# Sixteen partitions between the batch rows of a decode kernel's final sum, and two stacked copies in place of two side-by-side ones

## The chip, the cores and the metric

The kernel runs on one core of one Trainium2 chip. The metric is device time in microseconds (us) of the whole launch: the median over several runs. A profile covers one execution, and its span is the part of that execution in which the profiler saw instructions. TensorE is PE in the profile (PEld is its weight load), VectorE is DVE, ScalarE is ACT, GpSimd is POOL, SyncE is SP.

## The reference, cut to what matters

Two batch rows `x` of 448 values are normalized and go through an attention layer over the last 4096 positions of a long cache (16 query heads, 8 key/value heads of 256) and, next to it, through a dense layer with a mish activation. The result is the sum of three terms, two rows of 448 values:

```python
x = A_x                                  # 2 x 1 x 448, bfloat16
xn = _layernorm(x, axis=-1)
return x + _A_ref(xn, A_k_cache, A_v_cache, A_wq, A_wo) + _B_ref(xn, B_w1, B_b1, B_w2)
# _A_ref: q = xn @ wq;  p = softmax(q k^T / 16);  o = p v;  o (2 x 4096) @ wo (4096 x 448)
# _B_ref: h = xn @ w1 + b1;  act = h * tanh(softplus(h));  act (2 x 1792) @ w2 (1792 x 448)
```

## The kernel before

**Stages.** The work order is written out by hand in the body of the kernel (lines 651 to 743); no scheduler reorders it. Nearly all loads are issued by SP, in program order. First come `wq`, the first two key blocks (`load_k`, 4 MB each) and `w1`. `project` (L324) forms the queries, and the VectorE copies at L361 spread them into `qd`. Then a loop `u` over four groups of heads runs `turns` (VectorE transposes of the key block, L306), `scores` (TensorE, L393; ScalarE exponential, L401), `values` (TensorE, L439), `gather`, `finish`, `relay` and `mix_early`. The key, value, `wq` and `w2` blocks share a ring of three buffers, so a load waits until the block that lay there is used up.

**Set-up.** Before the first key block is transposed, GpSimd fills constants in program order (`ident`, `qd`, `ones`, `hot`, `pick_f`, `xs`, the `sp` tiles, `w2_x`), and VectorE makes small tables from `ident`, among them `id2`, a 2 x 2 identity in float32 (L145, L146).

**The final sum.** For the first three groups, the products with `wo` are added in `early` (2 x 448 in PSUM). For the last group and for the dense output the sum lies in `acc`, a PSUM tile of 224 columns: the left 224 output columns of the two batch rows lie on partitions 0 and 1, the right 224 on partitions 32 and 33. `carry` (L271) copies `early` to SBUF and brings it into `acc` through `id2`. `add_rows` (L284) issues one pair of matmuls for each 128 rows of weights, one into partitions 0 and 1 and one into 32 and 33; the stationary operand has two columns (batch rows), the moving operand 224 columns of weights. `mix` (L527) makes eight pairs from `ox` and `wo`; `dense_out` (L643) makes thirteen pairs from `act_bf` and `w2`. `w2` comes in five parts (`w2_parts`, L626), and the pairs of each part wait for that part. `relay` (L493) writes `ox`: in the last group ScalarE writes its partitions 0 to 63 and VectorE 64 to 127.

**The end.** After the last pair, VectorE copies partitions 0 and 1 and ScalarE partitions 32 and 33 of `acc` into the two halves of `res` (2 x 448, bfloat16), and SP stores `res` as two runs of 896 bytes:

```python
    res = consts.tile([Bsz, D], BF16)
    for g in range(SG):
        dst = res[:, g * SD : (g + 1) * SD]
        src = acc[32 * g : 32 * g + Bsz, :]
        if g % 2 == 0:
            nc.vector.tensor_copy(out=dst, in_=src)
        else:
            nc.scalar.copy(out=dst, in_=src)
    nc.sync.dma_start(out=out.flatten_outer_dims(), in_=res[:])
```

Of the kernel before, what the change touches and what calls it, by code (L numbers as in the profile page):

```python
# [9 lines left out]
ALU = mybir.AluOpType  # L10
AXIS = mybir.AxisListType
BF16 = mybir.dt.bfloat16
FP32 = mybir.dt.float32
# [4 lines left out]
def kernel(  # L18
# [13 lines left out]
    nc = tc.nc  # L32
    P = 128
# [5 lines left out]
    Bsz, Sq, D = A_x.shape  # L39
# [8 lines left out]
    U = Hkv // KU  # L48
# [13 lines left out]
    NI = F2 // P  # L62
    NR = NI - 1
# [16 lines left out]
    consts = ctx.enter_context(tc.tile_pool(name="consts", bufs=1))  # L80
    small = ctx.enter_context(tc.tile_pool(name="small", bufs=2))
# [46 lines left out]
    for lo, hi in ((0, HW // 2), (HW // 2, NS * HW // 2), (NS * HW // 2, NS * HW)):  # L128
# [6 lines left out]
    ident = consts.tile([P, P], BF16)  # L135
# [6 lines left out]
    nc.vector.tensor_copy(  # L142
        out=halves[:], in_=ident[0:2, 0:2].unsqueeze(2).to_broadcast([2, 2, Bsz])
    )
    id2 = consts.tile([Bsz, Bsz], FP32)  # L145
    nc.vector.tensor_copy(out=id2[:], in_=ident[0:Bsz, 0:Bsz])  # L146
    hot = consts.tile([P, KU, 4, rep, 32, KU], BF16)
    nc.gpsimd.memset(hot[:], 0.0)
    for k in range(KU):
        nc.gpsimd.tensor_copy(  # L150
            out=hot[:, k, :, :, :, k],
            in_=ident[:].rearrange("p (q y) -> p y q", y=4).unsqueeze(2)
# [11 lines left out]
        out=rstd[:], in_=mv[:, 1:2], func=ACT.Sqrt, bias=eps_t[:], scale=1.0  # L164
# [4 lines left out]
        out=xn_bf[:],  # L169
        in0=x_bf[:],  # L170
# [7 lines left out]
        out=parm[:], in_=ident[:].rearrange("p (a o) -> p o a", o=2), axis=AXIS.X, op=ALU.add  # L178
# [3 lines left out]
        out=jm[:],  # L182
        in_=ident[:].rearrange("p (a j h) -> p j a h", j=J, h=rep),
        axis=AXIS.XY,
        op=ALU.add,
    )
    nc.vector.tensor_scalar(
        out=jm[:], in0=jm[:], scalar1=-1.0, scalar2=29952.0, op0=ALU.add, op1=ALU.mult
# [3 lines left out]
        out=mneg[:], in_=jm[:].unsqueeze(1).to_broadcast([P, TH * 8, J])  # L192
    )
    sel = consts.tile([P, 2, NQ], FP32)
    for x in range(2):
        for w in range(4):
            at = 32 * w + (2 * (w % 2) + x) * NQ
            src = ident[:, at : at + NQ]
            if w == 0:
                nc.vector.tensor_copy(out=sel[:, x, :], in_=src)  # L200
            else:
                nc.vector.tensor_tensor(
                    out=sel[:, x, :], in0=sel[:, x, :], in1=src, op=ALU.add
# [9 lines left out]
        out=pick_f[0:QB, 0:12],  # L213
        in_=idb.rearrange("p (a s) -> p a s", s=XB),
        axis=AXIS.X,
        op=ALU.add,
    )
    nc.vector.tensor_reduce(
        out=pick_f[QB:P, XO:XP].rearrange("p (e r) -> p e r", r=4)[:, :, 0:2],
        in_=ida.rearrange("p (e r s) -> p e r s", r=2, s=XA),  # L220
        axis=AXIS.X,
        op=ALU.add,
    )
    nc.vector.tensor_reduce(
        out=pick_f[QB:P, XP : XP + XA],
        in_=ida.rearrange("p (a s) -> p s a", s=XA),
        axis=AXIS.X,
        op=ALU.add,
    )
    nc.vector.tensor_reduce(  # L230
        out=pick_f[0:QB, XP:],
        in_=idb.rearrange("p (a s) -> p s a", s=XB),
        axis=AXIS.X,
        op=ALU.add,
# [18 lines left out]
    for odd in range(2):  # L253
        for half in range(2):
            o = (half + odd) % 2
            nc.vector.tensor_scalar(
                out=xs[:, odd::2, half * Bsz : (half + 1) * Bsz],
                in0=xr_ps[:, odd::2, :],
# [9 lines left out]
    SG, SD = 2, D // 2  # L268
    acc = ps_a.tile([P, SD], FP32)

    def carry():  # L271
        e_sb = small.tile([P, 2 * Dh], FP32, tag="vs", name="e_sb", bufs=1)[0:Bsz, 0:D]
        nc.scalar.copy(out=e_sb, in_=early[:])
        for g in range(SG):
            nc.tensor.matmul(
                acc[32 * g : 32 * g + Bsz, :],
                lhsT=id2[:],
                rhs=e_sb[:, g * SD : (g + 1) * SD],
                start=True,
                stop=False,  # L280
                skip_group_check=True,
            )

    def add_rows(lhsT, rows, stop=False):  # L284
        for g in range(SG):
            nc.tensor.matmul(  # L286
                acc[32 * g : 32 * g + Bsz, :],
                lhsT=lhsT,
                rhs=rows[:, g * SD : (g + 1) * SD],
                start=False,  # L290
                stop=stop,
                skip_group_check=True,
            )
# [20 lines left out]
    for n in range(2):  # L314
        for e in range(2):
# [3 lines left out]
                out=sp[:],  # L319
                in_=ident[:, o : o + 63 : 2].unsqueeze(1).to_broadcast([P, G, 32]),  # L320
# [91 lines left out]
    state = {}  # L412
# [80 lines left out]
    def relay(u):  # L493
        oT = state.pop(("oT", u))
        ox_ps = ps_m.tile([P, 4, 2, rep, Bsz], FP32, tag="m", name="ox_ps")
        for y in range(4):
            for k in range(KU):
                nc.tensor.matmul(  # L498
                    ox_ps[:, y, :, :, :].rearrange("p c h b -> p (c h b)"),
                    lhsT=hot[:, k, y, :, :, :].rearrange("p h q k -> p (h q k)"),  # L500
                    rhs=oT[:, :, k * rep : (k + 1) * rep, :].rearrange("p c h b -> p c (h b)"),
                    start=(y == 0 and k == 0),
                    stop=(y == 3 and k == KU - 1),
                    skip_group_check=True,
                )
        ox = small.tile([P, 8, Bsz], BF16, tag="ox", name="ox")
        for h in range(rep):
            rows = slice(h * 64, (h + 1) * 64)
            copy = nc.vector.tensor_copy if u == U - 1 and h == 1 else nc.scalar.copy
            copy(  # L510
                out=ox[rows].rearrange("p (y c) b -> p y c b", c=2), in_=ox_ps[rows, :, :, h, :]
            )
        state["ox", u] = ox
# [11 lines left out]
            )  # L525

    def mix(u):  # L527
        ox = state.pop(("ox", u))
        w = wo_t.pop(u)[:].rearrange("p k h (c d) -> p (k h c) d", c=2)
        for i in range(8):  # L530
            add_rows(ox[:, i, :], w[:, i, :])

    act_bf = consts.tile([P, NI, 2, Bsz], BF16)
    dealt = consts.tile([P, XS, Bsz], BF16)
    act_x = consts.tile([XP, XS, Bsz], BF16)
    w2_x = consts.tile([XP, XS * D], BF16)
# [34 lines left out]
    def mish():  # L571
        h_ps = state.pop("h")
        shape = [P, NI, 2, Bsz]
        u_sb = consts.tile(shape, FP32, name="u_sb")
        nc.scalar.activation(out=u_sb[:], in_=h_ps[:], func=ACT.Exp)
        t_sb = consts.tile(shape, FP32, name="t_sb")
        nc.vector.scalar_tensor_tensor(
            out=t_sb[:], in0=u_sb[:], scalar=2.0, in1=u_sb[:], op0=ALU.add, op1=ALU.mult
        )
        den = consts.tile(shape, FP32, name="den_sb")  # L580
        nc.vector.tensor_scalar(
            out=den[:], in0=t_sb[:], scalar1=2.0, scalar2=None, op0=ALU.add
        )
        nc.vector.reciprocal(out=den[:], in_=den[:])
        nc.vector.tensor_tensor(out=t_sb[:], in0=t_sb[:], in1=den[:], op=ALU.mult)
        nc.vector.tensor_tensor(out=act_bf[:], in0=h_ps[:], in1=t_sb[:], op=ALU.mult)
        nc.vector.tensor_tensor(
            out=dealt[:],
            in0=act_bf[:, NR, 1, :].unsqueeze(1).to_broadcast([P, XS, Bsz]),
            in1=share[:].unsqueeze(2).to_broadcast([P, XS, Bsz]),  # L590
            op=ALU.mult,
        )
# [50 lines left out]
    def dense_out(part):  # L643
        k, lo, hi = w2_parts[part]
        for i in range(lo, hi):
            at = k * KH + i * D
            add_rows(
                act_bf[:, i, k, :], state["w2"][:, at : at + D], stop=(k == 1 and i == NR - 1)
            )

    load_w1()
# [18 lines left out]
    turns(0, 1)  # L670
    dense_in()
    mish()
    scores(0, 1)
    weigh(0)
    regroup()
    for u in range(U - 1):
        load_k(u + 1, 0)
        load_v(u, 0)
        load_k(u + 1, 1)
        load_v(u, 1)  # L680
        load_wo(u)
        if u == 0:
            load_xb(0)
            load_xb(1)
            load_xa(0)
        if u == 1:
            load_xb(2)
            load_xb(3)
            load_xa(1)
        turns(u + 1, 0)  # L690
        values(u, 0)
        scores(u + 1, 0)
        turns(u + 1, 1)
        if u == U - 2:
            pace(11, key=ktm[1][:, 0, 0, :, 0:16])
        values(u, 1)
        gather(u)
        finish(u)
        scores(u + 1, 1)
        relay(u)  # L700
        if u == U - 2:
            dense_x()
        mix_early(u)
        if u < U - 2:
            weigh(u + 1)
    u = U - 1
# [5 lines left out]
    for part in range(len(w2_parts)):  # L712
        load_w2(part)
    pace(3)
    carry()
    pace(5)
    values(u, 0)
# [9 lines left out]
    pace(1)  # L727
    finish(u)
    relay(u)
    pace(2)  # L730
    mix(u)
    for part in range(len(w2_parts)):
        dense_out(part)

    res = consts.tile([Bsz, D], BF16)
    for g in range(SG):
        dst = res[:, g * SD : (g + 1) * SD]
        src = acc[32 * g : 32 * g + Bsz, :]
        if g % 2 == 0:
            nc.vector.tensor_copy(out=dst, in_=src)  # L740
        else:
            nc.scalar.copy(out=dst, in_=src)
    nc.sync.dma_start(out=out.flatten_outer_dims(), in_=res[:])


# [28 lines left out]
```

## Time and profile before

| | us |
|---|---|
| median of 3 runs | 188.88 (188.82 to 189.43) |
| the profiled execution | 188.59 |
| its span | 186.8 |
| PE busy, share of the span | 88.9, 48% |
| DVE busy | 97.1, 52% |
| ACT busy | 12.6, 7% |
| POOL busy | 7.8, 4% |
| bytes moved | 77.78 MB, 416 GB/s over the span |
| last copies of `acc`, DVE L740 and ACT L742 | 0.377 and 0.337 |
| issue of the store, L743 | 0.273, from 184.81 |

The profiled execution is 1.8 us longer than its span, and 0.29 us below the median. Times inside the span are counted from its start. An entry of the timeline gives start, length, engine, line, operation, the tiles written and read, the shapes, and in brackets how long the engine was idle before it and what ended that.

### The profile page before, as it was taken

The page shows a single profiled execution, that of the slowest core. Times are in us where ns is not written, and L with a number is a line of the kernel's source. Part 1 is how long each engine was busy: PE and PEld are TensorE (multiplying, and loading weights), DVE is VectorE, ACT ScalarE, POOL GpSimd, SP SyncE. Part 2 cuts the span into 40 slices and gives each one's busy share as a digit, 9 for nine tenths or more (in the row PEclk, how much of TensorE's full clock was granted, in tenths as well). Part 3 has the DMA queues.
Part 4 walks back from the last instruction along what each step waited for, and adds up shares of the span by engine and source line. Part 5 has one row for each costly group of instructions (what it writes and reads, how often), then busy time and mean ns, then how long its engine had stood idle before and what let it go on. Part 6 is the DMA issues. An engine that isn't in the chain of part 4 may idle for free.

```text
span 186.8 us, 1974 instructions
## 1 busy us (share of the span) xinstructions
PE 88.9 (48%) x854; PEld 38.1 (20%) x854; DVE 97.1 (52%) x100; ACT 12.6 (7%) x27; POOL 7.8 (4%) x18
## 2 busy tenths in 40 slices
PE   0057015893209300783039101881059059899694
PEld 0022002541003100241013000330022013434353
DVE  6961798974792098028940296048920593040100
ACT  3004000101000100110000100110000000210100
POOL 8800000000000000000000000000000000000000
PEclk9999999955555855599555855798556756999999
DMA  6999999999999999999999999999999999999991
GB/s 207 442 475 442 407 435 405 452 446 444 414 421 421 432 449 389 472 442 442 414 435 418 449 435 401 468 446 407 421 435 428 442 449 421 449 389 430 403 406 73
DMA packets 4523, 77.78 MB, mean 416 GB/s; under 512 B 522, under 2 KB 912, under 8 KB 1956
## 3 DMA queue, kind: packets, MB, share of 16 engines
q1 hardware_dynamic: 4512, 77.67, 97.2%
q8 instruction: 6, 0.10, 0.2%
q14 instruction: 1, 0.01, 0.0%
q10 hardware_dynamic: 4, 0.00, 0.0%
HBM read 77.67 MB, written 0.00 MB: 416 GB/s over the span
## 4 chain that ended last, share of the span: by engine, by line
DMA 73%; DVE 12%; PE 9%; issue 3%; SPq 1%; ACT 0%
DMA k<-in_A_k_cache_dram 44%; DMA v<-in_A_v_cache_dram 29%; DVE kt L306 12%; PE pv L439 3%; PE acc L286 1%; PE sc L393 1%; PE early L519 1%; PE early L617 1%; PE o L472 1%; SPq L129 1%; PE pace L658 1%; PE o L457 1%; PE ox_ps L498 0%; SPq L102 0%; ACT vs L451 0%
## 5 line engine op out<-in xcount | busy, mean ns | idle before, releaser
L306 DVE STREAM_TRANSPOSE kt<-k 128x4096 f32<-128x4096 f32 x16 | 70.1, 4417 | 31.1 <-DMA k<-in_A_k_cache_dram 31.1
L439 PE MATMUL pv<-v,p 128*32 128x512 bf16 x244 | 23.2, 546 | 55.8 <-DMA v<-in_A_v_cache_dram 55.8
L393 PE MATMUL sc<-kt,qd 128*32 128x512 bf16 x256 | 22.6, 489 | 11.2 <-DVE kt L306 11.2
L439 PEld LDWEIGHTS <-p 128*32 128x32 bf16 x244 | 8.5, 124 | 68.4 <-issue 44.9
L658 PE MATMUL pace<-mneg,ident 128*128 128x512 bf16 x42 | 12.7, 440 | 0.0
L393 PEld LDWEIGHTS <-qd 128*32 128x32 bf16 x256 | 7.7, 114 | 24.1 <-issue 19.7
L484 DVE TENSOR_TENSOR oT<-o,rec 128x16 bf16<-128x16 f32 x4 | 0.7, 175 | 21.1 <-PE o L457 17.5
L404 DVE STREAM_TRANSPOSE p<-ex 128x512 bf16<-128x512 bf16 x8 | 5.2, 690 | 10.6 <-ACT ex L401 10.6
L401 ACT ACTIVATE ex<-sc 128x512 bf16<-128x512 f32 x8 | 4.8, 597 | 85.4 <-PE sc L393 85.4
L425 DVE TENSOR_REDUCE rec<-dn 128x8 f32<-128x512 f32 x4 | 2.8, 691 | 13.3 <-PE dn L417 13.3
L658 PEld LDWEIGHTS <-ident 128*128 128x128 bf16 x43 | 4.2, 111 | 13.7 <-DVE kt L306 7.8
L248 PE MATMUL xr_ps<-ident,xrows 2*128 2x2 bf16 x7 | 1.0, 182 | 11.2 <-DVE xrows L247 11.2
L451 ACT COPY vs<-pv 128x512 f32<-128x512 f32 x4 | 2.3, 586 | 54.0 <-PE pv L439 54.0
L519 PE MATMUL early<-wo,ox 128*2 128x448 bf16 x24 | 5.0, 352 | 1.3 <-ACT ox L510 1.3
L457 PE MATMUL o<-sel,vs 128*128 128x8 f32 x32 | 4.3, 262 | 2.1 <-ACT vs L451 2.1
L457 PEld LDWEIGHTS o<-sel,vs 128*128 128x128 f32 x32 | 4.2, 196 | 4.5 <-ACT vs L451 4.4
L417 PE MATMUL dn<-p,ones 128*128 128x512 bf16 x8 | 2.8, 438 | 3.8 <-DVE p L375 3.8
L382 PE MATMUL sc<-mneg,ident 128*128 128x512 bf16 x8 | 4.1, 516 | 0.0
L658 PE MATMUL pace<-kt,ident 128*128 128x512 bf16 x1 | 0.6, 609 | 7.3 <-DVE kt L306 7.3
L561 PE MATMUL h_ps<-xs,w 128*128 128x4 bf16 x49 | 3.3, 186 | 0.9 <-DMA w<-in_B_w_dram 0.9
L191 DVE CAST mneg<-jm 128x512 bf16<-128x512 f32 x1 | 3.5, 3481 | 0.0
L328 PE MATMUL q_ps<-wq,xs 128*32 128x512 bf16 x28 | 3.2, 627 | 0.4 <-issue 0.4
(85 smaller groups left out, 58.4 us busy)
## 6 DMA issues: line engine op xcount, KB each, us to landing
k<-in_A_k_cache_dram SPq DMA_DIRECT2D x8, 4096.0 KB, 26.4
v<-in_A_v_cache_dram SPq DMA_DIRECT2D x7, 4096.0 KB, 21.2
wo<-in_A_wo_dram SPq DMA_DIRECT2D x4, 896.0 KB, 21.5
v<-in_A_v_cache_dram SPq DMA_DIRECT2D x1, 2560.0 KB
wq<-in_A_wq_dram SPq DMA_DIRECT2D x1, 1792.0 KB, 10.2
w<-in_B_w_dram SPq DMA_DIRECT2D x1, 1568.0 KB
wq<-in_A_wq_dram SPq DMA_DIRECT2D x1, 1536.0 KB, 6.3
v<-in_A_v_cache_dram SPq DMA_DIRECT2D x1, 1024.0 KB
```

The lines of the kernel that those rows point to most:

```text
L191: nc.vector.tensor_copy(out=mneg[:], in_=jm[:].unsqueeze(1).to_broadcast([P, TH * 8, J]))
L306: nc.vector.transpose(out=kt[i][:, :, r, :, :], in_=t[:, r * KE : (r + 1) * KE].bitcast(FP32).rearrange("p (a c j) -> p a c j", c=P // (R ...
L328: nc.tensor.matmul(q_ps[32 * u : 32 * (u + 1), :], lhsT=xs[:, s, :], rhs=wq_t[s][:, u * 512 : (u + 1) * 512], start=(s == 0), stop=(s == N ...
L382: nc.tensor.matmul(sc[:].rearrange("p t c m -> p (t c m)"), lhsT=ident[:], rhs=mneg[:].rearrange("p a j -> p (a j)"), start=True, stop=Fal ...
L393: nc.tensor.matmul(sc[32 * w : 32 * (w + 1)].rearrange("p t c m -> p t (c m)"), lhsT=qd[:, u, 2 * n + e, :, :].rearrange("p g q -> p (g q) ...
L401: nc.scalar.activation(out=ex[:, :, :, i, :], in_=sc[:], func=ACT.Exp, scale=scale)
L404: nc.vector.transpose(out=p_all[:, :, h * TH : (h + 1) * TH, :].rearrange("p g t q -> p t g q"), in_=ex[:, h * TH : (h + 1) * TH].rearrang ...
L439: nc.tensor.matmul(pv[32 * w : 32 * (w + 1), :, :].rearrange("p x d -> p (x d)"), lhsT=p_run[:, g, 4 * a : 4 * a + 4, :].rearrange("p t q ...
L457: nc.tensor.matmul(po[:, c, :], lhsT=sb[:, x, c::2], rhs=sel[:, x, :], start=(x == 0 and c == 0), stop=(last and x == 1), skip_group_check ...
L519: nc.tensor.matmul(early[:], lhsT=ox[:, i, :], rhs=w[:, i, :], start=False, stop=(u == U - 2 and i == 7),)
L561: nc.tensor.matmul(h_ps[:, i, :, :].rearrange("p k b -> p (k b)"), lhsT=w1_v[:, s, cols], rhs=xs[:, s, 0 : 2 * Bsz], start=False, stop=(s ...
L658: nc.tensor.matmul(ps[:].rearrange("p t c m -> p (t c m)"), lhsT=ident[:], rhs=rhs, start=True, stop=True, skip_group_check=True,)
```

## The change

The batch rows of the final sum move from neighbouring partitions to partitions that lie 16 apart: 0 and 16 for the left half, 32 and 48 for the right. The stationary operands of the final sum get 17 columns: columns 0 and 16 hold the two batch rows, the 15 between hold zeros. They are now two fixed tiles that GpSimd fills with zeros once at the start, `act_w` and `ox_w`; `id2` has 32 columns and is also filled first. The activation (L586 before) and the last group's `ox` copies write into columns 0 and 16 of them. At the end one copy takes columns 0 to 111 of partitions 0 to 48 of `acc`, and the other columns 112 to 223 of the same partitions. `res` has 49 partitions of 224 columns, and the store takes partitions 0, 16, 32 and 48 of it, four runs of 448 bytes.

```diff
-    id2 = consts.tile([Bsz, Bsz], FP32)
-    nc.vector.tensor_copy(out=id2[:], in_=ident[0:Bsz, 0:Bsz])
+    BW = 17
+    id2 = consts.tile([Bsz, 32], FP32)
+    nc.gpsimd.memset(id2[:], 0.0)
+    nc.vector.tensor_copy(out=id2[:, 0:BW:16], in_=ident[0:Bsz, 0:Bsz])
+    act_w = consts.tile([P, NI, 2, BW], BF16)
+    nc.gpsimd.memset(act_w[:], 0.0)
+    act_bf = act_w[:, :, :, 0:BW:16]
+    ox_w = consts.tile([P, 8, BW], BF16)
+    nc.gpsimd.memset(ox_w[:], 0.0)
     hot = consts.tile([P, KU, 4, rep, 32, KU], BF16)
...
-                acc[32 * g : 32 * g + Bsz, :],
+                acc[32 * g : 32 * (g + 1), :],
                 lhsT=id2[:],
...
-                acc[32 * g : 32 * g + Bsz, :],
+                acc[32 * g : 32 * g + BW, :],
                 lhsT=lhsT,
...
-        ox = small.tile([P, 8, Bsz], BF16, tag="ox", name="ox")
+        if u == U - 1:
+            ox = ox_w[:, :, 0:BW:16]
+        else:
+            ox = small.tile([P, 8, Bsz], BF16, tag="ox", name="ox")[:]
...
-            add_rows(ox[:, i, :], w[:, i, :])
-
-    act_bf = consts.tile([P, NI, 2, Bsz], BF16)
+            add_rows(ox_w[:, i, :], w[:, i, :])
...
-        nc.vector.tensor_tensor(out=act_bf[:], in0=h_ps[:], in1=t_sb[:], op=ALU.mult)
+        nc.vector.tensor_tensor(out=act_bf, in0=h_ps[:], in1=t_sb[:], op=ALU.mult)
...
-                act_bf[:, i, k, :], state["w2"][:, at : at + D], stop=(k == 1 and i == NR - 1)
+                act_w[:, i, k, :], state["w2"][:, at : at + D], stop=(k == 1 and i == NR - 1)
...
-    res = consts.tile([Bsz, D], BF16)
-    for g in range(SG):
-        dst = res[:, g * SD : (g + 1) * SD]
-        src = acc[32 * g : 32 * g + Bsz, :]
-        if g % 2 == 0:
-            nc.vector.tensor_copy(out=dst, in_=src)
-        else:
-            nc.scalar.copy(out=dst, in_=src)
-    nc.sync.dma_start(out=out.flatten_outer_dims(), in_=res[:])
+    rows = 32 * (SG - 1) + BW
+    res = consts.tile([rows, SD], BF16)
+    nc.vector.tensor_copy(out=res[:, 0 : SD // 2], in_=acc[0:rows, 0 : SD // 2])
+    nc.scalar.copy(out=res[:, SD // 2 :], in_=acc[0:rows, SD // 2 :])
+    nc.sync.dma_start(
+        out=out.flatten_outer_dims().rearrange("b (g d) -> g b d", g=SG), in_=res[0:rows:16, :]
+    )
```

More of the change, by code (lines that the diff above doesn't have):

```diff
@@ L527, in mix @@
     def mix(u):
-        ox = state.pop(("ox", u))
+        state.pop(("ox", u))
         w = wo_t.pop(u)[:].rearrange("p k h (c d) -> p (k h c) d", c=2)
         for i in range(8):
-            add_rows(ox[:, i, :], w[:, i, :])
-    act_bf = consts.tile([P, NI, 2, Bsz], BF16)
+            add_rows(ox_w[:, i, :], w[:, i, :])
     dealt = consts.tile([P, XS, Bsz], BF16)
```

## The prediction

> **What bounds the kernel now.** I read the page's slices and its chain first, then the timeline of the last 5 us, then the start.
>
> ```profile
> DMA  6999999999999999999999999999999999999991
> ...
> DMA 73%; DVE 12%; PE 9%; issue 3%; SPq 1%; ACT 0%
> ```
>
> The DMA engines are full from the second of 40 slices to the last but one, and 73% of the chain that ended last is transfers. Bytes and issue order of all loads are the same after the change. So the body can move only if a load starts later, and otherwise only the two ends count: the set-up before the first transpose, and the tail after the last loaded byte. The tail, from the timeline:
>
> ```profile
> 181.64 0.17 ACT L510 CAST ox<-ox_ps 64x16 bf16<-64x16 f32 x1 [5.06 <-PE ox_ps L498]
> 181.64 0.18 DVE L510 CAST ox<-ox_ps 64x16 bf16<-64x16 f32 x1 [0.43 <-PE ox_ps L498]
> ...
> 181.98 0.93 PE L286 MATMUL acc<-wo,ox 128*2 128x224 bf16 x16
> ...
> 182.74 1.60 PE L286 MATMUL acc<-w,act_bf 128*2 128x224 bf16 x26
> 184.08 0.08 PEld L286 LDWEIGHTS <-act_bf 128*2 128x2 bf16 x1 [0.15 <-issue]
> 184.37 0.38 DVE L740 CAST res<-acc 2x224 bf16<-2x224 f32 x1 [2.56 <-PE acc L286]
> 184.41 0.34 ACT L742 CAST res<-acc 2x224 bf16<-2x224 f32 x1 [2.60 <-PE acc L286]
> 184.81 0.27 SPq L743 DMA_DIRECT2D out_dram<-res  x1
> ```
>
> The two last copies run side by side and both end at 184.75. The store is issued 0.06 later, and the span ends at 186.8, 1.72 after the issue is over. Everything from 184.37 on is on the path. Of the matmuls before it, the busy time by windows shows how they stand to the last load:
>
> ```profile
> 183.40:183.70 0.30, 0.30 (x10) 0.23 (x8) 1.00 0.27 90
> 183.70:184.00 0.30, 0.30 (x10) 0.22 (x5) 1.00 0.00 0
> ```
>
> The columns are the window, its length, PE and PEld busy, the granted clock, DMA share and GB/s. The last bytes of `w2` move before 183.7. In a timeline cut into steps of 0.03 us, the pairs start every 0.094 us (182.26, 182.36, 182.46, ...), which is 224 columns at 2.4 per ns; only two steps are longer, 183.32 to 183.46 and 183.84 to 184.08. These are the first pair of part 3 of `w2` and the pair of part 5, and in the instruction order each of them waits for its own load. So TensorE is 0.05 and 0.15 us ahead of the loads there, and 184.08 is set by the last load (my reading: the trace writes "issue" beside the 0.15).
>
> **The change, part by part.** The sum is made on the profiled execution, 188.59 us, which is its span of 186.8 and 1.79 around it; the median of the runs lies 0.29 higher, so I add the same difference to 188.88.
>
> Set-up. GpSimd gets three more memsets ahead of `hot`, `pick_f`, `xs` and the `sp` tiles. Rows of this trace:
>
> ```profile
> 2.13 0.20 POOL L140 MEMSET ones<- 128x128 bf16 x1
> 2.28 0.95 POOL L148 MEMSET hot<- 128x1024 bf16 x1
> ...
> 4.13 0.28 POOL L252 MEMSET xs<- 128x224 bf16 x1
> ```
>
> `act_w` (238 columns) is like `xs`, 0.30; `ox_w` (136) like `ones`, 0.20; `id2` (32) like the constant fills, 0.11: 0.61 by lengths, about 0.45 by starts, since they overlap. VectorE's second instruction, the copy into `id2`, now waits for GpSimd's memset, and all of layer norm, `xrows`, `xs`, `qT` and `qd` queues behind it on VectorE; TensorE's `project` waits for `xs`. Before, those first two VectorE copies already take until 3.25, when `hot` is filled, so I move the whole VectorE set-up by at most 0.61. Cover: the first transpose waits for its key block, not for set-up.
>
> ```profile
> 21.50 8.77 DVE L306 STREAM_TRANSPOSE kt<-k 128x4096 f32<-128x4096 f32 x2 [1.21 <-DMA k<-in_A_k_cache_dram]
> ```
>
> VectorE is idle for 1.21 before it and another 0.90 before the second key block (31.18). The third key load, which waits until `project` has used `wq` (16.25), is queued behind 13 MB and needs no exact start. Cost 0; were the cover gone, 0.45 to 0.61.
>
> Middle. The activation writes columns 0 and 16 instead of neighbours: 28 elements at 40.92, before 2.95 us in which VectorE waits for ScalarE. `carry` loads 32 columns instead of 2 and runs around 168.5, ahead of 1.67 us in which TensorE waits for values. Cost 0 for both.
>
> Last `ox` copies (0.17 and 0.18, on the path): the same 16 elements, spread out. The `qd` copies at L361 also write in pieces, 0.43 for 256 elements, and 0.18 + 240 x 0.001 is the same. Cost 0, at most 0.02.
>
> Loads of 17 columns, 42 in the tail. A load of 2 columns lasts 83 ns, one of 32 columns (L439, same clock) 96: 0.43 ns a column, so 6.5 ns for 15 more. At L439 four loads of 32 columns fit beside each step of four 512-column matmuls: steps start at 174.62, 174.84, 175.05, 175.27, that is 0.215 for 0.213 of columns. That is 54 ns a load, and here 47 ns are there for a smaller one. I take 0. If all 6.5 ns showed, it would be 0.27, of which the two waits for `w2` take back 0.20: 0.07.
>
> Last copies. As built, the ScalarE copy no longer waits for TensorE but for VectorE's copy, and the store for ScalarE's alone: the two stand one after the other. The trace of before shows no pair on the same partitions of one bank. Length: VectorE takes 0.177 for 16 columns and 0.377 for 224, so 0.27 for 112; ScalarE 0.166 and 0.337, so 0.245. A hand-over from VectorE to ScalarE is 0.04 in this trace (`mv` ends at 3.49, `rstd` starts at 3.53). VectorE now needs both matmuls of the last pair, so I let it start at 184.41, when ScalarE started. 184.41 + 0.27 + 0.04 + 0.245 = 184.97 against 184.75: +0.22. Bounds by the nearest rows: both as short as the 16-column copies and the start at 184.37, 0.00; both as long as the 224-column ones, +0.43.
>
> The Trainium skill (PSUM — Partial Sum Buffer, "PSUM bank collisions raise a hardware error") asks for an order between any two engines on the same bank and the same 32 partitions, reads against reads too, and lets different quadrants run at once. The 0.04 between L740 and L742 agrees with its second half; its first half speaks against this change: with it +0.22, without it about -0.07.
>
> Store. Four runs of 448 bytes from stepped partitions instead of two of 896. The nearest row is a load with four runs from stepped partitions:
>
> ```profile
> L607 SPq DMA_DIRECT2D w_x<-in_B_w_dram x4: 704/732/792, 58.5 to 97.8; - x4
> L613 SPq DMA_DIRECT2D w_x<-in_B_w_dram x2: 627/632/637, 60.0 to 98.5; - x2
> ```
>
> L613 takes 0.63 in a full queue, where its neighbour, the `wo` load, takes 0.56: +0.07, which I take. Bounds: 0 (at the empty queue of the start, 128 runs take 0.40, the store's two runs 0.27: about 1 ns a run) and +0.52 (0.79 against 0.27). The data move within one 0.2 us window at 3% of the engines, so twice the packets cost 0 to 0.1; I take 0.02.
>
> The Trainium skill (DMA: Bandwidth & Descriptors, "Specifications") says that transfers below 512 bytes are done as read-modify-write. No run so far has a store that short, and the page gives no price for one; it points to more than my 0.02.
>
> Sum: 0.22 + 0.07 + 0.02 = +0.31, a profiled execution of 188.90 and a median of 189.2. That is 0.16%. What a measurement of this kernel can tell from no change is about 0.3%, 0.57 us, so I count it as the same.
>
> **Rivals.** (1) Slower: the stepped store is dear at the end, where nothing hides it. Issue as L613 or L607, +0.36 to +0.46, with the copies and the packets +0.60 to +0.70: 189.5 to 189.6. For it: no cheaper stepped issue is in the trace. Against: those were issued in a full queue, and this queue is empty. It decides once the issue is over 0.60 long. (2) The change gains: the copies are half as long and cost no more together than one did, the store is unchanged. -0.11 to -0.07: 188.8; over 0.3% only by the runs' scatter. Against: the built order. (3) The 17-column loads sit on the path: +0.31 + 0.07 = 189.3, or 189.5 if the waits for `w2` take nothing back. Against: L439's steps.
>
> **How the numbers follow.** Forecast 0.50 (0.38 within 0.3%, 0.12 above, as the copies' bound of +0.43 and the runs' scatter of 188.82 to 189.43 reach there); rival 1 0.27 (0.22 above, 0.05 within); rival 2 0.15 (0.08 within, 0.07 below, the scatter again); rival 3 0.08 (0.03 within, 0.05 above). Sums: faster 0.07, same 0.54, slower 0.39. The range runs from rival 2 less 0.2 of scatter, 188.6, to the bounds of copies and issue together, 188.88 + 0.43 + 0.52, about 189.9.
>
> **What would show it.** Right: DVE's last copy near 0.27 and ACT's near 0.25 starting only after it; the store issued near 185.0 with 0.27 to 0.35; pair steps still 0.094; the first transpose still waiting for its key block, by 0.6 to 0.8 in place of 1.21. Wrong: both copies starting together (rival 2), an issue over 0.60 or a span end over 2.0 after it (rival 1), pair steps over 0.10 (rival 3), or VectorE busy up to the first transpose.

## The result and the profile after

The changed kernel takes 189.40 us (median of 13 runs, 189.19 to 189.59) against 188.66 for the kernel before in the same session (188.57 to 189.43): ratio 1.0036, 95% interval 1.0028 to 1.0043. That is 0.74 us or 0.4%: the interval stays clear of 1, so the changed kernel is slower, by about as much as the prediction's bound of 0.3%, which lies inside the interval. The ratios leave disturbed runs out and so can differ a little from those of the medians. The profiled execution has a span of 187.5 in place of 186.8. The tail in the timeline of the changed kernel, to be held against the one of before:

```profile
181.65 0.18 ACT L520 CAST ox_w<-ox_ps 64x16 bf16<-64x16 f32 x1 [5.07 <-PE ox_ps L505]
181.65 0.19 DVE L520 CAST ox_w<-ox_ps 64x16 bf16<-64x16 f32 x1 [0.43 <-PE ox_ps L505]
...
181.99 0.94 PE L293 MATMUL acc<-wo,ox_w 128*17 128x224 bf16 x16
...
182.76 1.58 PE L293 MATMUL acc<-w,act_w 128*17 128x224 bf16 x26
184.38 0.27 DVE L746 CAST res<-acc 49x112 bf16<-49x112 f32 x1 [2.55 <-PE acc L293]
184.69 0.24 ACT L747 CAST res<-acc 49x112 bf16<-49x112 f32 x1 [2.86 <-DVE res L746]
184.96 0.64 SPq L748 DMA_DIRECT2D out_dram<-res  x1
```

Up to the first of the last two copies the two executions agree within 0.02 us (184.38 and 184.37), after 181.65 and 181.64. So in these two executions all that is lost is lost behind the last matmul. The copies now stand in a row: ScalarE's releaser is VectorE's copy, no longer TensorE. The store is issued 0.15 later (184.96, before 184.81). The issue itself is 0.64 long, before 0.27. When its data move is read from the busy time by windows of 0.01 us (the last columns are clock, DMA share and GB/s). These are the first windows with data, before and after:

```profile
185.55:185.56 0.01, 0.00 (x0) 0.00 (x0) 0.00 (x0) 0.00 (x0) 0.00 (x0) 1.00 0.24 90
```

```profile
186.22:186.23 0.01, 0.00 (x0) 0.00 (x0) 0.00 (x0) 0.00 (x0) 0.00 (x0) 1.00 0.14 45
```

From the end of the issue to the first data it was 0.47 (185.08 to 185.55) and is 0.62 (185.60 to 186.22). From there to the end of the span it is 1.3 in both (1.25 and 1.28). The sum: 0.15 for the order of the copies, 0.37 for the longer issue, 0.15 for the later start of the data: 0.67 of the 0.7 by which the spans differ.

The start, after:

```profile
21.64 8.77 DVE L313 STREAM_TRANSPOSE kt<-k 128x4096 f32<-128x4096 f32 x2 [0.91 <-DMA k<-in_A_k_cache_dram]
```

VectorE's set-up runs 0.44 later (`mneg` starts at 5.65 in place of 5.21), and the first transpose still waits for its key block.

### The profile page after: what moved, and what is told of

It reads as the page before. It is cut to its first block, busy times and chain, and to the rows that moved or that the text cites. A ratio compares the mean times of both kernels' runs of the same rounds, so it can differ in the third digit from the quotient of the medians.

```text
span 187.5 us, 1977 instructions
## 1 busy us (share of the span) xinstructions
PE 91.1 (49%) x854; PEld 40.0 (21%) x854; DVE 97.2 (52%) x100; ACT 12.5 (7%) x27; POOL 8.2 (4%) x21
## 4 chain that ended last, share of the span: by engine, by line
DMA 50%; DVE 24%; PE 20%; ACT 2%; SPq 1%; issue 1%
DMA v<-in_A_v_cache_dram 35%; DVE kt L313 19%; DMA k<-in_A_k_cache_dram 15%; PE sc L400 6%; PE pv L446 5%; PE o L464 3%; DVE p L411 2%; PE acc L293 1%; PE dn L424 1%; DVE rec L432 1%; ACT ex L408 1%; ACT vs L458 1%; PE early L529 1%; PE early L626 1%; SPq L129 1%
## 5 line engine op out<-in xcount | busy, mean ns | idle before, releaser
L400 PE MATMUL sc<-kt,qd 128*32 128x512 bf16 x256 | 23.1, 503 | 10.8 <-DVE kt L313 10.8
L464 PE MATMUL o<-sel,vs 128*128 128x8 f32 x32 | 5.9, 311 | 2.1 <-ACT vs L458 2.1
L464 PEld LDWEIGHTS o<-sel,vs 128*128 128x128 f32 x32 | 5.7, 261 | 4.5 <-ACT vs L458 4.4
```

Source lines behind the costliest of these rows:

```text
L400: nc.tensor.matmul(sc[32 * w : 32 * (w + 1)].rearrange("p t c m -> p t (c m)"), lhsT=qd[:, u, 2 * n + e, :, :].rearrange("p g q -> p (g q) ...
L464: nc.tensor.matmul(po[:, c, :], lhsT=sb[:, x, c::2], rhs=sel[:, x, :], start=(x == 0 and c == 0), stop=(last and x == 1), skip_group_check ...
```

## The experiments

The questions: what makes the issue of the store dear (the step of 16 partitions, the four short runs, or the three-level address), what the order of the copies costs, and whether set-up and 17-column loads are free. An address has one level for each dimension that the store walks: row (or partition) and column make two, half, row and column make three. Each of the three sets of runs has its own runs of the kernel before: 188.62 in the first, 188.73 in the second, 188.67 in the third (medians). The four runs that leave parts of the output out (two with four adjacent partitions, the short runs, the gap) are one execution each; their issue lengths come from that one.

**First set: the form of the store, and the copies**

*Two levels in place of three.*

```diff
-        out=out.flatten_outer_dims().rearrange("b (g d) -> g b d", g=SG), in_=res[0:rows:16, :]
+        out=out.flatten_outer_dims().rearrange("b (g d) -> (b g) d", g=SG), in_=res[0:rows:16, :]
```

> The changed kernel with one edit: the output is addressed as four rows of 224 in a row (two levels: row, column) and not as half, row, column (three levels). Still four runs of 448 bytes from partitions 0, 16, 32, 48. The right half of batch row 0 and the left half of row 1 land in each other's place. Theory levels (the three-level address makes the issue dear): issue of the store near 0.27 us in place of 0.64, data 0.4 us after the issue ends, about 0.54 us less than the changed kernel: near 188.9. Theory step (partitions 16 apart make it dear) and theory runs (four short runs make it dear): issue stays at 0.64, time stays at 189.4.

Measured: issue 0.61, 189.22 against 188.62 (ratio 1.0032, 1.0019 to 1.0045). Taking the third level away does not make the stepped store cheap. The theory of levels falls as the only cause.

*Four adjacent partitions, three levels.*

```diff
-    rows = 32 * (SG - 1) + BW
-    res = consts.tile([rows, SD], BF16)
-    nc.vector.tensor_copy(out=res[:, 0 : SD // 2], in_=acc[0:rows, 0 : SD // 2])
-    nc.scalar.copy(out=res[:, SD // 2 :], in_=acc[0:rows, SD // 2 :])
+    res = consts.tile([4, SD], BF16)
+    nc.vector.tensor_copy(out=res[:, :], in_=acc[0:4, :])
     nc.sync.dma_start(
-        out=out.flatten_outer_dims().rearrange("b (g d) -> g b d", g=SG), in_=res[0:rows:16, :]
+        out=out.flatten_outer_dims().rearrange("b (g d) -> g b d", g=SG), in_=res[:, :]
```

> The changed kernel with one VectorE copy of partitions 0 to 3 (224 columns) and a store of four adjacent partitions with the three-level address; the right half of the output and row 1 are left out (zeros and row 0 are stored). Theory levels: issue 0.64. Theory step: issue 0.27. Theory runs: issue 0.64. Under all three the copy ends at about 184.75 and the store is issued at 184.82.

One line on the store's issue (length in ns, minimum, median and maximum):

```profile
L746 SPq DMA_DIRECT2D out_dram<-res x1: 729/729/729, 184.7 to 184.7; - x1
```

Measured: issue 0.73. Taking the step away does not make it cheap either. So the theory of the step falls as the only cause too, and runs remained, unless step and third level are each enough.

*Two runs of 896 bytes, step kept.* Besides `res` and the store, the right half of the sum goes to a second PSUM bank, so that the two copies can stand side by side. No run has copies of 17 partitions, 32 apart, in one bank.

```diff
-                acc[32 * g : 32 * g + BW, :],
+                accs[g][32 * g : 32 * g + BW, :],
...
+    res = consts.tile([BW, D], BF16)
+    nc.vector.tensor_copy(out=res[:, 0:SD], in_=accs[0][0:BW, :])
+    nc.scalar.copy(out=res[:, SD:], in_=accs[1][32 : 32 + BW, :])
+    nc.sync.dma_start(out=out.flatten_outer_dims(), in_=res[0:BW:16, :])
```

> The changed kernel up to the last pair, but the right half of the sum in a second PSUM bank, so that VectorE and ScalarE copy 17 partitions x 224 columns side by side, into a tile with rows on partitions 0 and 16; the store has two runs of 896 bytes and a two-level address, as before the change, and only the step of 16 partitions is new. Theory step: issue 0.64, near 189.2. Theories levels and runs: issue 0.27 from 184.81, and the whole execution as the kernel before, 188.7 (within 0.1), since set-up, 17-column loads and second bank cost nothing. If set-up or loads cost something after all, it stays above 188.8 with a cheap issue.

```profile
L749 SPq DMA_DIRECT2D out_dram<-res x1: 700/700/700, 185.0 to 185.0; - x1
```

Measured: issue 0.70, 189.34 (ratio 1.0033, 1.0022 to 1.0045). Against the kernel before, this store differs in the step alone, so the step alone is enough to make it dear. Long runs do not help.

*Copies side by side, the store of the change.*

```diff
-    nc.vector.tensor_copy(out=res[:, 0 : SD // 2], in_=acc[0:rows, 0 : SD // 2])
-    nc.scalar.copy(out=res[:, SD // 2 :], in_=acc[0:rows, SD // 2 :])
+    nc.vector.tensor_copy(out=res[0:BW, :], in_=accs[0][0:BW, :])
+    nc.scalar.copy(out=res[32:rows, :], in_=accs[1][32:rows, :])
```

> The changed kernel with the right half of the sum in a second PSUM bank and the copies side by side (17 partitions x 224 columns each); the store is that of the change. If the order of the two copies costs what the trace shows (store issued at 184.96 against 184.81), this is 0.15 us under the changed kernel, near 189.25, with both copies ending near 184.75 and the issue still 0.64. Rival: copies of 17 partitions are longer than of 2, then it is no faster.

The timeline of its end:

```profile
184.38 0.38 DVE L748 CAST res<-acc 17x224 bf16<-17x224 f32 x1 [2.48 <-PE acc_r L295]
184.42 0.34 ACT L749 CAST res<-acc_r 17x224 bf16<-17x224 f32 x1 [2.52 <-PE acc_r L295]
184.83 0.64 SPq L750 DMA_DIRECT2D out_dram<-res  x1
```

Measured: 189.12 (ratio 1.0028, 1.0018 to 1.0038), +0.50 over the kernel before, where the changed kernel has +0.66 to +0.74. Copies of 17 partitions are as long as copies of 2 (0.38 and 0.34), both start at once, and the store is issued 0.13 earlier than in the changed kernel. By the traces the order of the copies is worth this 0.13 to 0.15, and the rest is the store. The times agree with that but do not show it alone: the interval overlaps that of the changed kernel (1.0028 to 1.0043), and the run before, whose copies stand side by side too, lost 0.72.

**Second set: plain stores, two stores, one copy**

*Adjacent and flat.* The run with four adjacent partitions, with this edit:

```diff
-        out=out.flatten_outer_dims().rearrange("b (g d) -> g b d", g=SG), in_=res[:, :]
+        out=out.flatten_outer_dims().rearrange("b (g d) -> (b g) d", g=SG), in_=res[:, :]
```

> As the run with four adjacent partitions (one VectorE copy of partitions 0 to 3, three of the four quarters of the output left out), but the output is addressed as four rows of 224 in a row. Four runs of 448 bytes, no step, no third level. Theory plain (an issue is cheap only when partitions are adjacent and the address has two levels; a step or a third level each makes it dear): issue 0.27 and data 0.4 after its end. Theory runs of this form (more than two partitions, or runs under 512 bytes, are dear, and the step is dear by itself): issue 0.6 to 0.7.

```profile
L746 SPq DMA_DIRECT2D out_dram<-res x1: 289/289/289, 184.9 to 184.9; - x1
```

```profile
185.63:185.64 0.01, 0.00 (x0) 0.00 (x0) 0.00 (x0) 0.00 (x0) 0.00 (x0) 1.00 0.14 45
```

Measured: issue 0.29 from 184.87, data from 185.63, span 186.9. Four runs of 448 bytes from four partitions cost the same within 0.02 as two of 896, in the issue, in the wait for the data (0.47) and from there to the end (1.3). Neither the number of runs nor their length is what is dear. Against the run with four adjacent partitions and three levels, a two-level address is all that changed: 0.73 becomes 0.29.

*Short runs from two adjacent partitions.* An edit of the kernel before:

```diff
-    nc.sync.dma_start(out=out.flatten_outer_dims(), in_=res[:])
+    keep = 200
+    nc.sync.dma_start(
+        out=out.flatten_outer_dims().rearrange("b (g d) -> b g d", g=SG)[:, :, 0:keep],
+        in_=res[:].rearrange("b (g d) -> b g d", g=SG)[:, :, 0:keep],
+    )
```

> The kernel before with one edit: from each half row of 224 only 200 columns are stored, so that two adjacent partitions give four runs of 400 bytes with a gap between; 24 columns of each half are left out. Copies as before, store issued at 184.81. Theory plain: the partitions are adjacent but the tile side has a third level, so issue 0.6 to 0.7. Theory step alone: 0.27. Under both the data-to-end time stays 1.25 if short runs cost nothing once they move.

```profile
L744 SPq DMA_DIRECT2D out_dram<-res x1: 756/756/756, 184.8 to 184.8; - x1
```

```profile
186.14:186.15 0.01, 0.00 (x0) 0.00 (x0) 0.00 (x0) 0.00 (x0) 0.00 (x0) 1.00 0.13 40
```

Measured: issue 0.76, data from 186.14, 0.63 after the issue, and again 1.3 to the end of the span (187.4). The partitions are adjacent; a third level, here written on both sides of the store, is enough by itself.

*Two stores.*

```diff
-    nc.sync.dma_start(
-        out=out.flatten_outer_dims().rearrange("b (g d) -> g b d", g=SG), in_=res[0:rows:16, :]
-    )
+    o2 = out.flatten_outer_dims()
+    nc.sync.dma_start(out=o2[:, 0:SD], in_=res[0:BW:16, :])
+    nc.sync.dma_start(out=o2[:, SD:], in_=res[32:rows:16, :])
```

> The changed kernel with two stores from SP in a row in place of one: partitions 0 and 16 to the left halves, then 32 and 48 to the right halves, two runs of 448 bytes each, two-level addresses. Theory step: each issue takes 0.64, so the span is 0.6 longer than the changed kernel's, near 190.0. Theory first use (the first dear form after a long time pays for something that the second finds ready): first 0.64, second near 0.27 to 0.4, near 189.7. If runs or levels were what is dear, both take 0.27 and it is no slower than 189.4.

```profile
184.84 0.70 SPq L749 DMA_DIRECT2D out_dram<-res  x1
185.58 0.63 SPq L750 DMA_DIRECT2D out_dram<-res  x1
```

Measured: 0.70 and 0.63, 189.97 against 188.73 (ratio 1.0076, 1.0059 to 1.0094). The second stepped store pays nearly the full price again, so it is not paid once for a first use, and the two issues on SP did not overlap (the first ends at 185.54, the second starts at 185.58).

*One copy.*

```diff
-    nc.vector.tensor_copy(out=res[:, 0 : SD // 2], in_=acc[0:rows, 0 : SD // 2])
-    nc.scalar.copy(out=res[:, SD // 2 :], in_=acc[0:rows, SD // 2 :])
+    nc.vector.tensor_copy(out=res[:, :], in_=acc[0:rows, :])
```

> The changed kernel with one VectorE copy of 49 partitions x 224 columns in place of the two that stand one after the other. 0.38 in place of 0.27 + 0.04 + 0.24, so the store is issued at 184.82 in place of 184.96, its issue stays 0.64: 0.14 under the changed kernel, as with copies side by side (189.12). If the hand-over between the engines cost nothing, it is equal to the changed kernel, 189.4.

```profile
184.39 0.38 DVE L746 CAST res<-acc 49x224 bf16<-49x224 f32 x1 [2.55 <-PE acc L293]
184.80 0.64 SPq L747 DMA_DIRECT2D out_dram<-res  x1
```

The trace agrees: one copy of 0.38, and the store 0.16 earlier than in the changed kernel. The times do not decide it: 189.32 (189.09 to 189.53) against 188.73 is +0.59, between the two expectations.

**Third set: the rest of the change, and what a cheap issue needs**

*The changed kernel again*, no edit.

> The changed kernel itself, unedited, beside the other three: near 189.4, issue 0.64, 0.7 above the kernel before.

Measured: 189.33 against 188.67 (ratio 1.0035, 1.0023 to 1.0047), issue 0.64.

*The change without its end.* The last copies, `res` and the store as before the change, and

```diff
-    nc.vector.tensor_copy(out=id2[:, 0:BW:16], in_=ident[0:Bsz, 0:Bsz])
+    nc.vector.tensor_copy(out=id2[:, 0:Bsz], in_=ident[0:Bsz, 0:Bsz])
...
-    act_bf = act_w[:, :, :, 0:BW:16]
+    act_bf = act_w[:, :, :, 0:Bsz]
...
-            ox = ox_w[:, :, 0:BW:16]
+            ox = ox_w[:, :, 0:Bsz]
```

> The change without its end: fixed operands of 17 columns, the three memsets and the 32-column carry as in the change, but the batch rows in columns 0 and 1, and copies, tile and store as before. Theory end (all of the loss lies behind the last matmul): equal to the kernel before, within 0.1 us, issue 0.27. Rival set-up and loads (they cost something that one trace does not show): above it by 0.1 to 0.3.

```profile
L293 PEld LDWEIGHTS <-act_w x26: 86/92/93, 182.8 to 184.2; 128*17 128x17 bf16 x26
```

Measured: 188.81 (188.59 to 189.07) against 188.67, ratio 0.9999 (0.9981 to 1.0017). The medians are 0.14 apart, the ratio shows no difference and holds either sign within 0.2%. The loads of 17 columns take 92 ns in place of 84. The issue is 0.27 again. So the loss of 0.7 is in the end; of set-up, loads and the wider carry together 0.1 to 0.2 can't be excluded by the times of this run. All the traces together narrow it: the first of the last copies starts at 184.27 to 184.60 in the ten with the changed set-up and operands (mean 184.43), and at 184.31 to 184.54 in the four without them (mean 184.44). That the two executions shown at first agree within 0.02 is partly luck, then, but there is no shift.

*A gap between the rows.* An edit of the kernel before:

```diff
-    nc.sync.dma_start(out=out.flatten_outer_dims(), in_=res[:])
+    nc.sync.dma_start(out=out.flatten_outer_dims()[:, 0:400], in_=res[:, 0:400])
```

> The kernel before, storing only 400 of the 448 columns of each row (48 columns are left out): adjacent partitions, two levels, two runs of 800 bytes with a gap in the output. If adjacent partitions and two levels are all that a cheap issue needs: 0.27 to 0.29. If the output must also be without gaps: 0.6 to 0.76.

```profile
L743 SPq DMA_DIRECT2D out_dram<-res x1: 273/273/273, 185.0 to 185.0; - x1
```

Measured: issue 0.27. The output may have gaps; adjacent partitions and two levels were enough.

*The store issued by ScalarE.* An edit of the kernel before:

```diff
-    nc.sync.dma_start(out=out.flatten_outer_dims(), in_=res[:])
+    nc.scalar.dma_start(out=out.flatten_outer_dims(), in_=res[:])
```

> The kernel before with the store issued by ScalarE, which does the last copy itself. If the issue costs the same there, it starts up to 0.06 us earlier: 188.6, no difference that can be told. If ScalarE's queue is slower (its one load at the start took 0.52 to issue): up to 0.25 more.

Measured: issue 0.25 in place of 0.27, 188.69 against 188.67 (ratio 1.0009, 0.9992 to 1.0026). No difference. No run points to a version that beats the kernel before.

## Why the prediction was right or wrong

The median, 189.40, lies in the range, but the likeliest case gave 189.2 and "same" by the bound of 0.3%. What happened is rival 1: it priced the issue at +0.36 to +0.46 (measured +0.37) and the whole at +0.60 to +0.70 (0.7 by the spans, 0.74 and 0.66 by the medians). Of its two signs one came (the issue is over 0.60), the other did not: the span ends 1.9 after the issue, not over 2.0. That its total fits so well is partly luck, as it took the copies 0.07 too dear and the start of the data 0.13 too cheap.

- **Body, set-up, loads, `ox` copies, carry: 0.** Right, as far as the scatter lets it be seen. The set-up moved by 0.44, just under the 0.45 to 0.61 given, and the transpose still waits for its key block: 0.91 here, where I expected 0.6 to 0.8, and 0.60 to 1.39 over the ten traces with the new set-up. From the first pair of `mix` to the first of `dense_out`, eight pairs, it is 0.77 (181.99 to 182.76) where it was 0.76, so the longer weight loads stay hidden, which speaks against rival 3. `carry` stood at 166.85 and not around 168.5 as I read it; nothing hangs on that.
- **Last copies: +0.22.** Right in mechanism, 0.07 too much. The lengths were 0.27 and 0.24 as worked out, and the hand-over 0.04. But VectorE started at 184.38 and not at 184.41, and SP followed ScalarE's copy after 0.03 and not 0.06. The rule of the Trainium skill (PSUM — Partial Sum Buffer, "PSUM bank collisions raise a hardware error") named this cost: same bank and same partitions stand in order here, and with a second bank the copies ran side by side. Two readers at once in one place were not tried, nor what builds this order.
- **Store issue: +0.07.** The step that failed. I took the difference between L613 and the `wo` load beside it, both in a full queue, and put it on top of 0.27 from the empty one. But the neighbour is no plain row: in the kernel's code the `wo` load has a three-level address itself (`y k (i d)`). The runs show that the price of this store goes with its form: 0.61 to 0.76 for every store with a step or a third level in an empty queue, about as much as L613 and L607 (partitions 4 apart) in a full one (0.63 to 0.79); 0.25 to 0.29 for the plain ones (adjacent partitions, two levels). The whole length of the nearest row was the price, not its excess over a neighbour.
- **Packets: +0.02.** Too small by 0.13, and for another reason than the one weighed. The data started 0.62 after the issue in place of 0.47, and the same in the other dear forms, with long runs or adjacent partitions too (0.62 to 0.63), while four short plain runs started after 0.47. The wait goes with the form too.
- **Runs under 512 bytes.** The rule of the Trainium skill (DMA: Bandwidth & Descriptors, "Specifications") shows no price here: with runs of 400, 448, 800 and 896 bytes alike the span ends 1.2 to 1.3 after the first data.

Why a step or a third level costs more is not settled by these runs, only that either does; of steps, the stores had 16 partitions only.

## What to carry to other kernels

A last store is paid in full, so its form counts: keep its rows on adjacent partitions with a two-level address on both sides. Here two copies side by side and a plain store were 0.59 faster than one copy and a stepped store. Price an operation by the whole duration of the row of the same form, not by what that row differs from its neighbours in another state of the queue; and take that as an estimate, since a row of the same form elsewhere can differ too (below). Before two engines share a copy, see that they do not read the same partitions of one PSUM bank; here the halves then came one after the other.

## What the runs showed of the hardware that was not expected

The issue of this last store of 1.6 to 1.8 KB took 0.25 to 0.29 us with adjacent partitions and two levels, and 0.61 to 0.76 with a step of 16 partitions or a third level; the data then started about 0.15 later after the end of the issue, too. The number of runs (two or four) and their length made no difference of more than 0.02 to the plain store. This is shown for a last store only: the load of `x` at the start, two rows of 896 bytes on adjacent partitions with two levels, took 0.52 to issue on ScalarE, and why is open:

```profile
L123 ACTq DMA_DIRECT2D x_bf<-in_A_x_dram x1: 517/517/517, 0.7 to 0.7; - x1
```

A VectorE copy of 224 columns out of PSUM took 0.38 on 2, 4, 17 and 49 partitions alike.
